# Column tiles on TensorE for two products of a gated attention kernel, with its work list laid out anew

## The chip, the cores and the metric

The kernel runs on one core of one Trainium2 chip. A time is the device time of one execution in microseconds (us). The profile comes from one execution, and its span runs from the first to the last instruction of the program.

A core has five engines that run side by side, each taking its own instructions in order: TensorE (PE in the profile; its loads of stationary operands, called weights here, are shown apart as PEld), VectorE (DVE), ScalarE (ACT), GpSimd (POOL) and SyncE (SP), which here only issues transfers. TensorE writes its results to PSUM, a memory of eight banks for each of 128 partitions, and another engine has to carry them from there to the large on-chip memory before the bank is used again.

## What is computed

There are two attention layers over the same input `x` (2048 tokens, 640 features, 32 heads of 20), and a gate for each token that mixes them. Layer A is a linear attention with softmax features of both signs:

```python
pk = einsum('bhsd,hdf->bhsf', k, w_phi)
phi_k = concatenate([softmax(pk), softmax(-pk)], axis=-1)
kv = einsum('bhsf,bhsd->bhfd', phi_k, v)
z = einsum('bhsf->bhf', phi_k)
num = einsum('bhqf,bhfd->bhqd', phi_q, kv)
den = einsum('bhqf,bhf->bhq', phi_q, z)[..., None] + 1e-06
a = (num / den) @ wo
```

Layer B works in four segments of 512 tokens. Within a segment it is causal softmax attention; beside it, features of the queries read a memory of the earlier segments, and both are mixed by a gate for each head. The result is `g * a + (1 - g) * b`. The change touches only `kv` and `z` of layer A.

## The kernel before

All matrices lie with 128 rows in the partitions. The key features of layer A are in `phk`, a tile of 128 x (16 token chunks, 640 features, 2 signs) in bf16, so that the features of one sign are every second element. The values of layer A are in `vA` (16 chunks x 640).

Every piece of work is a short function with numbered steps. The order is one hand-over list of words, `ORDER` (before: lines 838 to 898): the first letter names the function, the first digit its step, a second digit the PSUM bank, and an `a` that ScalarE carries the result from PSUM in place of VectorE. The loop behind the list calls the functions word by word, and as program order is kept on each engine, the list fixes the order in which each engine and each transfer queue works. Buffers and the waits between engines follow from the tiles that the steps read and write.

The words that matter here:

- `A` and `B`: key features and values of layer A, chunk by chunk. `B` reads the weights `WvA`.
- `S` (function `sums`, L357): `z` in blocks. The reference sums 2048 features in bf16, and the kernel follows that rounding: sums over blocks of 32 tokens come from TensorE, and VectorE adds the 64 blocks in order. In step 0, each 128 x 128 piece of `phk` is the weights and `ind` (128 x 4, one column for each block of 32 rows) is streamed: 40 matmuls of 4 columns in a step, 160 in all, into `zb_ps`. Step 1 copies a sign's result to `zt`, with the features already in the partitions.
- `s` (`blocks`, L372): 35 small VectorE operations, the running sums `zh` over the blocks and what is made of them for the denominators (`HZ`).
- `X` (`products`, L384): `kv`. For each of five groups of 128 features and each sign, 16 matmuls (one for each token chunk) with 128 x 128 weights from `phk` and 140 or 160 columns of `vA`: all heads that the group's 128 features touch. A head mask `hm` then clears what belongs to other heads when VectorE copies `kv_ps` to `KV`.
- `P` (`scores`) and `U` (`attended_cols`): the scores of layer B (`st_ps`), their exponentials on ScalarE (`PT`), and the attended values. `U` already uses four column tiles: the output of head i goes to partitions 32 i to 32 i + 31 (`uv_ps`). Its result is turned by a transfer (`U2`, `uN`), whose first reader is a reciprocal on VectorE (`U3`, `rden`). From the fourth on, all scores use one group of four banks, so a score step waits for the exponential of the one before it.
- `k`, `v`, `q`, `f`: projections, `o`: output projections; `d` and `n`: denominators and numerators of layer A; `M`: the memory of layer B.

Until about 60 us the list holds mainly loads, `A` and `B`; the `S` and `X` steps lie between 67 and 96 us, among the first score steps; then follow projections, scores and outputs until the end. `R0` closes the tiles of the first part, `phk`, `vA` and `WvA` among them, once `X` is done.

Of the kernel before, what the change touches and what calls it, by code (L numbers as in the profile page):

```python
# [8 lines left out]
ALU = mybir.AluOpType  # L9
# [6 lines left out]
def kernel(  # L16
# [192 lines left out]

    gps.memset(Msb, 0.0)  # L210
# [7 lines left out]
    ind = const.tile([P, 4], BF16, name="ind")  # L218
# [5 lines left out]
    zt = apool.tile([P, 2 * KC, 2, 32], BF16, name="zt")  # L224
# [9 lines left out]
    def item(kind, n):  # L234
        if (kind, n) not in items:
            items[kind, n] = It()
        return items[kind, n]
# [69 lines left out]
    def masks(n, step, at, ev):  # L307
        if step == 0:
            vec.tensor_tensor(
                out=Wphi, in0=Wc[:, :, None, :].to_broadcast([P, KC, NW, DH]),  # L310
                in1=hn_f[:, :, :, None].to_broadcast([P, KC, NW, DH]), op=ALU.mult)
            return
        if step == 1:
            vec.tensor_copy(out=hm, in_=hn_f)
        elif step == 2:
            vec.tensor_copy(out=ind, in_=bd01)
        else:
            vec.tensor_copy(out=HZ[:, :, step - 3, 0, :], in_=hm)
# [37 lines left out]

    def sums(n, step, at, ev):  # L357
        sgn, half = divmod(n, 2)
        t = item("S", sgn)
        if step == 0:  # L360
            if half == 0:
                t.ps = bank([P, KC, 4 * NCH], "zb_ps", at)
            for sc in range(half * NCH // 2, (half + 1) * NCH // 2):
                for c in range(KC):
                    ten.matmul(t.ps[:, c, 4 * sc:4 * sc + 4], lhsT=phk[:, sc, c * P:(c + 1) * P, sgn],
                               rhs=ind, start=(sc == 0 and c == 0),
                               stop=(sc == NCH - 1 and c == KC - 1), skip_group_check=True)
        else:
            vec.tensor_copy(
                out=zt[:, sgn * KC:(sgn + 1) * KC].rearrange("p c h k -> p c (h k)"), in_=t.ps)  # L370

    def blocks(n, step, at, ev):  # L372
        if n == 0:
            vec.tensor_copy(out=zh, in_=zt[:, :, :, 0])
        elif n < 32:
            vec.tensor_tensor(out=zh, in0=zh, in1=zt[:, :, :, n], op=ALU.add)
# [7 lines left out]
    def products(n, step, at, ev):  # L384
# [3 lines left out]
        if step == 0:  # L388
            t.ps = bank([P, hi - lo, DH], "kv_ps", at)
            for sc in range(NCH):  # L390
                ten.matmul(t.ps, lhsT=phk[:, sc, c * P:(c + 1) * P, sgn],
                           rhs=vA[:, sc, lo * DH:hi * DH],
                           start=(sc == 0), stop=(sc == NCH - 1))
# [423 lines left out]
    def tail_out(j, step, at, ev):  # L817
# [15 lines left out]
    WHICH = {**{f"V{j}": lambda i: i + UL for j in range(5)}, "k2": lambda i: 2 * i + 1, "o2": lambda i: 2 * i + 1, "S1": lambda i: 2 * i + 1,  # L833
# [103 lines left out]
```

## Time and profile before

| | us |
|---|---|
| median of 3 runs (291.45 to 294.0) | 291.5 |
| the profiled execution | 292.36 |
| its span | 290.6 |
| VectorE busy | 239.8 |
| ScalarE busy | 239.6 |
| GpSimd busy | 183.8 |
| busy with `zb_ps` (160 matmuls, 67.7 to 78.8 us) | 4.6 |
| busy with `kv_ps` (160 matmuls, 81.3 to 95.7 us) | 11.2 |

Engines work at the same time, so busy times are not added. A matmul's recorded length includes the time until its result has left the array, and the next one starts long before: what a step costs on TensorE is read from the distance of the starts, which the chain of work shows as the length of a piece. The clock granted to TensorE is 1.00 of full speed in all of the span.

### The profile page before, as it was taken

How to read it: one execution, taken by the hardware profiler on the slowest of the kernel's cores; microseconds unless marked ns; L12 is line 12 of the kernel's file. 1: busy time of each engine (PE TensorE's matmuls, PEld its weight loads, DVE VectorE, ACT ScalarE, POOL GpSimd, SP SyncE). 2: the span in 40 equal slices, each digit the busy share in tenths (PEclk: the TensorE clock that was granted, in tenths of full speed). 3: DMA queues.
4: the chain of work that ended last, by engine and by line, in shares of the span. 5: the costliest groups of instructions: out<-in, count | busy, mean ns of one | idle time of the engine just before them, and what ended most of it. 6: DMA issues, size and time to landing. Idle time of an engine off the chain costs nothing.

```text
span 290.6 us, 8207 instructions
## 1 busy us (share of the span) xinstructions
PE 278.1 (96%) x3233; PEld 176.2 (61%) x3233; DVE 239.8 (83%) x576; ACT 239.6 (82%) x260; POOL 183.8 (63%) x305
## 2 busy tenths in 40 slices
PE   8999999999999999999999999999999999898994
PEld 4676666667677546565546556556555555566673
DVE  5969999999699539999889988798898769989613
ACT  2478976998867899999999988999899998888801
POOL 8050000037346846797996899989789996998610
PEclk9999999999999999999999999999999999999999
DMA  7999960100110694546243425141736114356422
GB/s 226 252 237 215 166 142 11 36 2 20 20 20 20 203 158 89 72 86 134 39 92 72 106 58 104 39 106 36 124 72 139 26 41 111 83 122 126 106 62 90
DMA packets 79591, 28.10 MB, mean 97 GB/s; under 512 B 69952, under 2 KB 79552, under 8 KB 79552
## 3 DMA queue, kind: packets, MB, share of 16 engines
q1 hardware_dynamic: 78608, 26.84, 45.3%
q10 hardware_dynamic: 944, 0.74, 0.8%
q8 instruction: 25, 0.41, 0.6%
q14 instruction: 14, 0.11, 0.1%
HBM read 5.61 MB, written 2.62 MB: 28 GB/s over the span
## 4 chain that ended last, share of the span: by engine, by line
PE 66%; ACT 18%; DMA 5%; DVE 4%; POOL 3%; issue 3%; DVEq 0%; ACTq 0%; SPq 0%; POOLq 0%
ACT PT L117 15%; PE o_ps L117 9%; PE proj L117 8%; PE v_ps L117 8%; PE k_ps L117 8%; PE st_ps L117 7%; PE pf_ps L117 6%; PE q_ps L117 6%; PE uv_ps L117 4%; PE kv_ps L117 4%; DMA phk<-in_A_wqkv_dram 3%; PE mem_ps L117 2%; PE num_ps L117 2%; ACT ET L117 2%; PE zb_ps L117 1%
## 5 line engine op out<-in xcount | busy, mean ns | idle before, releaser
L117 ACT ACTIVATE PT<-st_ps 128x2048 bf16<-128x2048 f32 (+1 forms) x83 | 151.2, 1826 | 18.5 <-PE st_ps L117 14.0
L117 POOL TENSOR_SCALAR_AFFINE_SELECT PT<-PT 128x512 bf16<-128x512 bf16 (+2 forms) x116 | 80.5, 708 | 37.7 <-ACT PT L117 37.2
L117 PEld LDWEIGHTS <-xT 128*128 128x128 bf16 x640 | 59.5, 98 | 28.4 <-issue 5.7
L117 PE MATMUL st_ps<-qTp,kTs 32*128 32x384 bf16 (+3 forms) x512 | 31.8, 300 | 5.0 <-ACT PT L117 4.7
L117 ACT ACTIVATE Ek<-k_ps 128x640 bf16<-128x640 f32 x32 | 26.2, 893 | 6.2 <-PE k_ps L117 4.3
L117 POOL TENSOR_TENSOR Msb<-Msb,mtmp 128x84 f32<-128x84 f32 x24 | 9.3, 386 | 33.9 <-DVE mtmp L117 33.7
L117 DVE TENSOR_TENSOR t<-num_ps,dd 128x320 f32<-128x320 f32 x64 | 28.0, 481 | 2.3 <-POOL oA L117 1.3
L117 POOL TENSOR_TENSOR oA<-t,t 128x320 bf16<-128x320 f32 x32 | 29.1, 914 | 0.9 <-DVE t L117 0.7
L117 PEld LDWEIGHTS <-oT 128*128 128x128 bf16 x240 | 22.2, 98 | 10.4 <-issue 2.2
L117 PEld LDWEIGHTS <-kTs 32*128 32x128 bf16 (+1 forms) x552 | 14.8, 92 | 20.3 <-issue 16.3
L117 PE MATMUL proj<-WvB,xT 128*128 128x320 bf16 x160 | 26.2, 300 | 0.2 <-ACT vB L117 0.2
L117 PE MATMUL proj<-WkB,xT 128*128 128x320 bf16 x160 | 25.9, 300 | 0.0
L117 PE MATMUL q_ps<-xT,WqB 128*128 128x512 bf16 x100 | 24.9, 380 | 0.0
L117 PE MATMUL pf_ps<-xT,WqA 128*128 128x512 bf16 x100 | 24.9, 379 | 0.0
L117 PE MATMUL v_ps<-WvA,xT 128*128 128x320 bf16 (+1 forms) x160 | 24.5, 300 | 0.0
L117 PE MATMUL k_ps<-qTp,xT 128*128 128x320 bf16 x160 | 23.7, 299 | 0.1
L117 DVE TENSOR_REDUCE ksum<-Ek 128x64 f32<-128x1280 bf16 x16 | 23.3, 1455 | 0.0
L117 ACT ACTIVATE ET<-pf_ps 128x512 bf16<-128x512 f32 x40 | 22.0, 627 | 0.0
L117 POOL TENSOR_TENSOR oB<-td,tm 128x320 bf16<-128x320 f32 (+4 forms) x25 | 20.8, 835 | 0.4
L117 PE MATMUL o_ps<-WoA,oT 128*128 128x320 bf16 x120 | 20.3, 300 | 0.3 <-DVE tm L117 0.3
L117 PE MATMUL uv_ps<-PT,vB 128*32 128x512 bf16 (+1 forms) x448 | 20.4, 302 | 0.1
L117 PEld LDWEIGHTS <-phk 128*128 128x128 bf16 x370 | 17.6, 98 | 4.4 <-DMA phk<-in_A_x_dram 1.7
(115 smaller groups left out, 490.0 us busy)
## 6 DMA issues: line engine op xcount, KB each, us to landing
out_dram<-osb SPq DMA_DIRECT2D x12, 160.0 KB
qTp<-qd SPq DMA_DIRECT2D x8, 128.0 KB
WvB<-in_B_wv_dram SPq DMA_DIRECT2D x1, 800.0 KB
vA<-in_B_wq_dram SPq DMA_DIRECT2D x1, 800.0 KB
WvA<-in_A_wqkv_dram SPq DMA_DIRECT2D x1, 800.0 KB
WoA<-in_A_wo_dram SPq DMA_DIRECT2D x1, 800.0 KB
WoB<-in_B_wo_dram SPq DMA_DIRECT2D x1, 800.0 KB
qTp<-qd SPq DMA_DIRECT2D x8, 96.0 KB
```

What stands on the lines that cost most here:

```text
L117: return lambda *a, **k: kept(f(*a, **k))
```

## The change

It has three parts.

**Block sums.** The roles are exchanged: `ind` becomes the weights and `phk` is streamed, 320 features of one sign at a time. There are four steps (two halves of the features, two signs) with 16 matmuls each, in four column tiles: chunk 4 q + u goes to column tile q, that is to partitions 32 q to 32 q + 31, and the weights of u are 32 columns of which only 4 u to 4 u + 3 are not zero, so that four chunks add up into the same tile without touching each other's rows. Now the blocks are in the partitions and the features along the row, so the result goes to `zb` and one transfer turns it to `zt` (step 2). Both take the place of `WvA`, which is not needed any more by then. The running sums read other columns of `zt`.

```diff
+    ind = apool.tile([P, 144], BF16, name="ind")
+    gps.memset(ind, 0.0)
...
+    WvF = WvA.rearrange("p c n -> p (c n)")
+    zb = WvF[:, 0:2 * D].rearrange("p (s n) -> p s n", s=2)
+    zt = WvF[:, 2 * D:4 * D].rearrange("p (c n) -> p c n", n=P)
+    ztv = zt.rearrange("p c (h k) -> p c h k", h=2)
...
-            vec.tensor_copy(out=ind, in_=bd01)
+            vec.tensor_copy(out=ind.rearrange("p (u k) -> p u k", k=36)[:, :, 0:4],
+                            in_=bd01[:, None, :].to_broadcast([P, 4, 4]))
...
     def sums(n, step, at, ev):
+        if step == 2:
+            syn.dma_start_transpose(out=zt, in_=zb.rearrange("p s n -> p (s n)"))
+            return
         sgn, half = divmod(n, 2)
-        t = item("S", sgn)
-        if step == 0:
-            if half == 0:
-                t.ps = bank([P, KC, 4 * NCH], "zb_ps", at)
-            for sc in range(half * NCH // 2, (half + 1) * NCH // 2):
-                for c in range(KC):
-                    ten.matmul(t.ps[:, c, 4 * sc:4 * sc + 4], lhsT=phk[:, sc, c * P:(c + 1) * P, sgn],
-                               rhs=ind, start=(sc == 0 and c == 0),
-                               stop=(sc == NCH - 1 and c == KC - 1), skip_group_check=True)
-        else:
-            vec.tensor_copy(
-                out=zt[:, sgn * KC:(sgn + 1) * KC].rearrange("p c h k -> p c (h k)"), in_=t.ps)
+        t = item("S", n)
+        if step == 0:
+            t.ps = bank([P, 320], "zb_ps", at)
+            for u in range(4):
+                for q in range(4):
+                    ten.matmul(t.ps[32 * q:32 * q + 32, :], lhsT=ind[:, 32 * u:32 * u + 32],
+                               rhs=phk[:, 4 * q + u, half * 320:(half + 1) * 320, sgn],
+                               start=(u == 0), stop=(u == 3), tile_position=(0, 32 * q),
+                               skip_group_check=True)
+        else:
+            ev(out=zb[:, sgn, half * 320:(half + 1) * 320], in_=t.ps)
```

**Products.** Each 128 x 128 matmul of `X` becomes two with 64 columns of weights, in two column tiles (partitions 0 to 63 and 64 to 127 of the result). Each streams only the heads that its 64 features touch, 80 columns; the first chunk still streams all 140 or 160, which sets the whole region.

```diff
             for sc in range(NCH):
-                ten.matmul(t.ps, lhsT=phk[:, sc, c * P:(c + 1) * P, sgn],
-                           rhs=vA[:, sc, lo * DH:hi * DH],
-                           start=(sc == 0), stop=(sc == NCH - 1))
+                for f in range(c * P, (c + 1) * P, 64):
+                    a, b = (lo, hi) if sc == 0 else (f // DH, -(-(f + 64) // DH))
+                    r = f - c * P
+                    ten.matmul(t.ps[r:r + 64, a - lo:b - lo, :], lhsT=phk[:, sc, f:f + 64, sgn],
+                               rhs=vA[:, sc, a * DH:b * DH], start=(sc == 0), stop=(sc == NCH - 1),
+                               tile_position=(0, r), skip_group_check=True)
```

**The list.** All 1,600 words are put in a new order. Besides the `S` words the same steps are in it as often; some results are carried by another engine (four of `o` and two of `q` go from ScalarE to VectorE; one of `T`, one of `v` and two of the last outputs `h` go the other way, and ScalarE carries one of the four block sums). The part around the new steps, in which `S2` is the new transfer and `s0` a running sum:

```diff
-        "q2 B03 B3a A3 P1 B12 P2 S00 P3 B4 A5 B2a P4 P01 G0 B3a k01 B4 A4 P1 G1 B03 A5 P2 P3 B12 "
-        "G2 k1 B2 S0 K0 P4 G3 B3a K1 B4 P01 O0 S1 U01 P1 B03 U1 B12 U2 B2 G0 P3 P00 G1 S00 B3a B4 "
-        "G2 P1 G3 B01 B13 B2 P3 P00 U3 B3 S0 P1 B4 U4 B02 U5 S1 B11 s0 B2 P3 s0 P00 B3 U03 B4 s0 "
-        "s0 X00 s0 P1 U1 s0 U2 X02 s0 X1 s0 s0 s0 P3 P00 s0 X01 P1 X1 X03 s0 X1 s0 s0 s0 U3 P3 "
...
+        "P1 B4 B11 B2 U00 B3 B4 P3 P00 U1 J0 S03 P1 J4 U2 J1 B02 J2 J3 J5 B11 B2a O0 P3 P00 B3 "
+        "S00 S1a B4 P1 S02 U3 S1 U4 S01 U5 S1 U03 S1 G0 P3 P00 S2 U1 X00 P1 G1 G2 X02 G3 X1 X01 "
+        "X1 P3 P00 X1 M03 P1 f00 M6 U2 M7 k02 s0 s0 s0 s0 P3 P00 k1 X01 P1 s0 X03 U3 s0 X1 U4 s0 "
+        "U5 U02 s0 G0 X1 P3 P00 s0 X01 U1a G1 s0 G2 P1 s0 G3 U2 s0 X03 X1 s0 s0 X02 s0 X1 s0 s0 "
```

More of the change, by code (lines that the diff above doesn't have):

```diff
@@ L217 @@
     hm = const.tile([P, KC, NW], BF16, name="hm")
-    ind = const.tile([P, 4], BF16, name="ind")
     rgS = const.tile([P, NCH], F32, name="rgS")
@@ L223 @@
     CM = const.tile([P, G, 4, DH + 1], BF16, name="CM")
-    zt = apool.tile([P, 2 * KC, 2, 32], BF16, name="zt")
+    WvF = WvA.rearrange("p c n -> p (c n)")
+    zb = WvF[:, 0:2 * D].rearrange("p (s n) -> p s n", s=2)
+    zt = WvF[:, 2 * D:4 * D].rearrange("p (c n) -> p c n", n=P)
+    ztv = zt.rearrange("p c (h k) -> p c h k", h=2)
     zh = apool.tile([P, 2 * KC, 2], BF16, name="zh")
@@ L357, in sums @@
     def sums(n, step, at, ev):
+        if step == 2:
+            syn.dma_start_transpose(out=zt, in_=zb.rearrange("p s n -> p (s n)"))
+            return
         sgn, half = divmod(n, 2)
-        t = item("S", sgn)
+        t = item("S", n)
         if step == 0:
-            if half == 0:
-                t.ps = bank([P, KC, 4 * NCH], "zb_ps", at)
-            for sc in range(half * NCH // 2, (half + 1) * NCH // 2):
-                for c in range(KC):
-                    ten.matmul(t.ps[:, c, 4 * sc:4 * sc + 4], lhsT=phk[:, sc, c * P:(c + 1) * P, sgn],
-                               rhs=ind, start=(sc == 0 and c == 0),
-                               stop=(sc == NCH - 1 and c == KC - 1), skip_group_check=True)
-        else:
-            vec.tensor_copy(
-                out=zt[:, sgn * KC:(sgn + 1) * KC].rearrange("p c h k -> p c (h k)"), in_=t.ps)
+            t.ps = bank([P, 320], "zb_ps", at)
[5 more added lines that the diff above has]
+                               skip_group_check=True)
+        else:
+            ev(out=zb[:, sgn, half * 320:(half + 1) * 320], in_=t.ps)
     def blocks(n, step, at, ev):
         if n == 0:
-            vec.tensor_copy(out=zh, in_=zt[:, :, :, 0])
+            vec.tensor_copy(out=zh, in_=ztv[:, :, :, 0])
         elif n < 32:
-            vec.tensor_tensor(out=zh, in0=zh, in1=zt[:, :, :, n], op=ALU.add)
+            vec.tensor_tensor(out=zh, in0=zh, in1=ztv[:, :, :, 32 * (n // 16) + n % 16], op=ALU.add)
         elif n == 32:
@@ L832 @@
                  p=tail_first, a=tail_mid, e=tail_next, z=tail_last)
-    WHICH = {**{f"V{j}": lambda i: i + UL for j in range(5)}, "k2": lambda i: 2 * i + 1, "o2": lambda i: 2 * i + 1, "S1": lambda i: 2 * i + 1,
+    WHICH = {**{f"V{j}": lambda i: i + UL for j in range(5)}, "k2": lambda i: 2 * i + 1, "o2": lambda i: 2 * i + 1,
              **{f"M{j}": lambda i: i + G for j in range(2, 6)}, "p1": lambda i: 3 * i}
     ORDER = (
[60 rows of a table removed]
[61 rows of a table added]
     done = {}
```

113 rows, old and new, of the table ORDER are left out of this document.

## The prediction, as it was put on record

> **What bounds the kernel now.** I read the busy shares first, then the same busy times cut into four stages, then the chain of work that ended last, then the groups of instructions with their shapes apart, and the waits last. The profiled execution took 292.36 us (span 290.6 us and 1.76 us around it). The median of the three runs is 291.5 us, 0.86 us less, so a saving found in this profile is taken off 291.5.
>
> ```profile
> PE 278.1 (96%) x3233; PEld 176.2 (61%) x3233; DVE 239.8 (83%) x576; ACT 239.6 (82%) x260; POOL 183.8 (63%) x305
> ...
> PE 66%; ACT 18%; DMA 5%; DVE 4%; POOL 3%; issue 3%; DVEq 0%; ACTq 0%; SPq 0%; POOLq 0%
> ```
>
> ```profile
> core 0: us, PE busy (x) PEld busy (x) DVE busy (x) ACT busy (x) POOL busy (x), PEclk, DMA share, GB/s
> 0.00:20.00 20.00, 18.23 (x144) 12.32 (x145) 15.09 (x34) 9.57 (x16) 9.57 (x24) 1.00 0.95 245
> 20.00:110.00 90.00, 89.84 (x990) 59.98 (x989) 76.06 (x170) 73.95 (x102) 29.73 (x50) 1.00 0.47 86
> 110.00:274.00 164.00, 157.17 (x1975) 94.76 (x1977) 143.93 (x363) 152.99 (x140) 141.78 (x229) 1.00 0.43 87
> 274.00:290.60 16.60, 12.84 (x132) 9.18 (x131) 4.73 (x12) 3.04 (x4) 2.76 (x5) 1.00 0.22 67
> ```
>
> TensorE is what sets the end. It is busy 278.1 of 290.6 us, and its 12.5 us of idle time lie in three places: 1.8 us in the first 20 us (first loads), 6.8 us from 110 to 274, and 3.8 us behind the last matmul and in the tail. From 20 to 110 us, where both steps that the change rewrites lie, it is idle for 0.16 us. So work taken off TensorE there moves everything after it. From 110 to 274 us ScalarE is nearly as full (152.99 of 164, 93%), so there the time of either counts.
>
> The chain shows the steps in order (start, length, engine and output, matmuls):
>
> ```profile
> 69.96 1.37 PE v_ps L117 x10
> 71.32 0.98 PE zb_ps L117 x40
> 72.30 0.33 PE st_ps L117 x4
> 72.63 0.66 PE uv_ps L117 x16
> 73.29 1.47 PE v_ps L117 x10
> 74.76 0.33 PE st_ps L117 x8
> 75.09 1.09 PE zb_ps L117 x40
> ...
> 81.35 2.05 PE kv_ps L117 x32
> 83.40 0.33 PE st_ps L117 x8
> 83.73 2.05 PE kv_ps L117 x32
> ...
> 86.37 1.11 PE kv_ps L117 x16
> ...
> 88.57 2.19 PE kv_ps L117 x32
> ...
> 91.09 1.08 PE kv_ps L117 x16
> ...
> 93.84 2.05 PE kv_ps L117 x32
> ```
>
> Three prices come out of it. A block-sum matmul (`zb_ps`) costs 0.98/40 = 24.5 ns although it streams only 4 columns: that is what one load of 128x128 weights with one short matmul takes, and it also says that such a load fits into 24.5 ns. Steps that change the way the array is divided cost about 0.10 us more (`v_ps` 1.47 before a score step against 1.37 before a block-sum step, `zb_ps` 1.09 against 0.98). And `uv_ps`, which already runs as four column tiles, streams 512+384+256+128 = 1280 columns in each tile in 0.66 us: one tile after the other would be 5120 columns, so the four run side by side, at 0.56 us and one change of 0.10.
>
> **Block sums, part by part.** Before, 160 matmuls in four groups: 4 x 0.98 = 3.9 us, without changes of division. After, four steps of 16 matmuls, four tiles side by side with 4 x 320 = 1280 columns each, the same as `uv_ps`: 4 x 0.56 = 2.2 us. In the new list three of the four stand between a score step and a `uv_ps` step, with no change more; the first stands between a score step and a value projection, one change more, 0.1. Together 2.3, a saving of 1.6 us. The streamed operand is now every second element of `phk`; no row shows such a stream. If it went at half rate the steps would take 4.5 us, 0.6 more than before; I take full rate, because the only rows with this stride (`phk` as weights, below) show loads as quick as those without it, and keep 2.2 us in the range.
>
> ```profile
> L117 PE MATMUL zb_ps<-ind,phk 128*128 128x4 bf16 x160 | 4.6, 164 | 0.0
> ...
> L117 PEld LDWEIGHTS <-xT 128*128 128x128 bf16 x640 | 59.5, 98 | 28.4 <-issue 5.7 <-DVE osb L117 0.2
> ...
> L117 PEld LDWEIGHTS <-phk 128*128 128x128 bf16 x370 | 17.6, 98 | 4.4 <-DMA phk<-in_A_x_dram 1.7 <-issue 1.5 <-DMA phk<-in_A_wqkv_dram 0.8
> ...
> L117 PEld LDWEIGHTS <-vB 128*32 128x32 bf16 x448 | 9.5, 96 | 11.1 <-issue 3.1 <-DVE t L117 1.1 <-DVE rden L117 0.3
> ```
>
> The evacuation grows from two casts to three on VectorE and one on ScalarE:
>
> ```profile
> L117 DVE CAST zt<-zb_ps 128x320 bf16<-128x320 f32 x2 | 1.0, 489 | 0.9 <-PE zb_ps L117 0.9
> ```
>
> That is 0.49 us more on VectorE, which is idle 90 - 76.1 = 14 us between 20 and 110 us; nothing on the path. The new transfer that turns the sums goes into SP's queue behind the first `uN` transfer and ahead of the second; it waits for the last of the four casts, which stands just ahead of it in the list. The nearest transfer takes 2.86 us for 512 columns:
>
> ```profile
> 118.16 2.86 DMA uN<-uT
> ```
>
> For 1280 columns that is 2.86 us if its length doesn't matter and 7.2 us if it goes by columns. Between it and the first running sum the list puts three products, a score step, a memory step, a feature projection and a key projection, about 4.8 us of TensorE's work. So VectorE's queue, with the product evacuations behind those sums, waits 0 to 2.4 us; I take 0, since from 512 to 1280 columns the fixed part stays, and keep 2.4. The result is wanted by the denominators some 25 us later. The clear of the larger `ind` is one short memset on an idle GpSimd.
>
> **The products.** Before: 2.05 x 3 + 2.19 + 1.11 + 1.08 = 10.5 us, of which six changes of division are 0.6: 9.9 us for 160 matmuls, 62 ns each. After: 320 matmuls, in 16 rounds of two tiles for each of ten products, 80 columns instead of 140 (all 140 or 160 in the first round). A round lasts as long as the longer of its stream and its weight load. The stream:
>
> ```profile
> 211.43 0.32 PE num_ps L117 x6
> ```
>
> Six matmuls of 4 x 140 + 2 x 80 = 720 columns in 0.32 us are 0.44 ns a column, 36 ns for 80 columns. The load is the unknown: 64 columns of weights into each of two tiles, while no row shows a column tile whose stream is short enough to show its load. Lower end: hidden, 36 ns. Middle: a round issues two pairs of a load and a matmul, and 24.5 ns is the shortest turn of such a pair in any row, so 49 ns if the two tiles' pairs follow one another. Upper end: each of the two loads takes twice the whole 128-column load, 98 ns. The ten products then take 10 x (16 x r + 0.03): 6.1, 8.1 or 16.0 us. I take 49 ns, since a turn bound by its load is what `zb_ps` shows and `uv_ps` with its long streams doesn't, so 8.1 us and a saving of 1.8 us; the ends are a saving of 3.8 and a loss of 6.1.
>
> [...]
>
> **The list.** The steps of TensorE are the same in number apart from these two kinds, so the new list can change the end only by TensorE's idle time.
>
> ```profile
> L117 ACT CAST qd<-q_ps 128x512 bf16<-128x512 f32 x8 | 4.7, 586 | 0.0
> ...
> L117 ACT CAST osb<-o_ps 128x320 bf16<-128x320 f32 x8 | 3.4, 425 | 0.5 <-PE o_ps L117 0.5
> ```
>
> It gives VectorE six copies that ScalarE had (4 of `osb`, 2 of `qd`), 0.43 and 0.59 us each, about 3 us, taken from an engine at 93% and put on one with 20 us idle in the same stage. It puts the score steps at the same distance: by the step lengths of the chain some 192 us of TensorE's work lie between the fourth and the last of 80 in the old list, 2.5 us for each. In the tail TensorE has no gap after 278.14 in either list, but the last evacuation goes from two casts in a row to one:
>
> ```profile
> 278.14 8.17 PE o_ps L117 x60
> 286.34 0.89 DVE vB L117 x2
> ```
>
> That is 0.3 us less, since the last matmul runs beside the first of the two. For 110 to 274 us I take the idle time as it is, 6.8 us; what a new list can win or lose there I put at 2.5 us either way, about a third of it.
>
> Sum: -1.6 (block sums) -1.8 (products) -0.3 (last evacuation) = -3.7 us; 292.36 becomes 288.7, and the median 291.5 - 3.7 = 287.8 us.
>
> **Rivals.** First, another bound takes the place of TensorE. The score steps share one group of four banks, so each waits for the exponential before it:
>
> ```profile
> PE st_ps L117 <- ACT PT L117: 4.7, 16, 0.6
> ...
> DVE rden L117 <- DMA uN<-uT: 3.6, 2, 3.3
> ```
>
> ```profile
> L117 ACT ACTIVATE PT<-st_ps 128x2048 bf16<-128x2048 f32 x77 | 145.4, 1888 | 18.3 <-PE st_ps L117 14.0 <-PE uv_ps L117 1.3 <-POOL Mbd L117 0.6
> ```
>
> One turn is 1.89 + 0.40 us and hand-overs, 2.4 us, and the list has 2.5 us of TensorE's work for it. If quicker products only lengthen that wait, 1.8 us are lost again: 289.6 us. For it speaks ScalarE's 93%, against it that in the products' stage ScalarE still has 90 - 74 = 16 us idle. Chance 0.27.
>
> Second, slower: the new list reads the turned columns sooner. Adding TensorE's steps between a `uN` transfer and its reader (the reciprocal `rden` on VectorE), the median over 28 units falls from 3.5 to 2.9 us and now meets the 2.86 us of the transfer. A reader that comes too early stops VectorE, with key, value and numerator evacuations queued behind it, and then TensorE's banks. With half of the units late by 0.5 us that is 7 us: 287.8 + 7 = 294.8 us. It decides once VectorE, idle 12% of that stage, reaches the reader before the landing; the old list shows it twice, for 3.6 us. Chance 0.13.
>
> Third, slower: weight loads in column tiles are not hidden behind the streams, or are twice as long. Then a round is 36 + 49 = 85 to 98 ns, the products take 13.9 to 16.0 us, and the time is 291.5 - 1.6 - 0.3 + 4.0 to 6.1 = 293.6 to 295.7 us. [...] Against it stand these rows of the plain and the tiled form, loads beside the matmuls of the same rows:
>
> ```profile
> 72.56 0.50 PEld L117 LDWEIGHTS <-vB 128*32 128x32 bf16 x16 [0.23 <-DVE omgb L117]
> 72.56 0.73 PE L117 MATMUL uv_ps<-PT,vB 128*32 128x512 bf16 x16
> ```
>
> Chance 0.10.
>
> **The numbers.** The forecast has 0.50. Its own range is 284.5 (loads hidden, a little less idle) to 289.5. A measurement of this kernel can tell about 1% from no change, 2.9 us: faster means under 288.6, slower over 294.4. Faster: 0.45 of the forecast and 0.03 of the first rival. Within 1%: 0.05 and 0.24, and 0.05 of the two slow cases near their lower ends. Slower: 0.18. The range leaves out the upper half of the slow cases and a few in a hundred below: 284.5 to 294.5.
>
> **What would show it.** `zb_ps` as four groups of 16 at 0.55 to 0.66 us, and `kv_ps` at 32 matmuls in 0.8 to 0.9 us a product, say the terms are right; 0.6 says the loads are hidden, 1.4 or more is the third rival. TensorE idle between 110 and 274 us well over 6.8 us, with VectorE waiting for `uN`, is the second; a wait of scores for exponentials well over 4.7 us is the first. A running sum waiting for its transfer, or block sums at twice 0.56, would break the cover or the stream rate that I assumed.

## The result and the profile after

The changed kernel takes 293.86 us (median of 20 runs, 291.92 to 295.81) against 291.71 us for the kernel before (20 runs beside it). The ratio is 1.0063, with a 95% interval of 1.0045 to 1.0080: about 2 us slower, where 3.7 us less were forecast. Its profiled execution took 293.18 us with a span of 291.5 us. The two profiled executions lie only 0.8 us apart (292.36 and 293.18), so the traces hold less than half of the 2.15 us between the two medians; where the rest lies is not shown.

The busy times of the engines and the chain's shares by engine, after:

```profile
PE 273.7 (94%) x3276; PEld 171.0 (59%) x3297; DVE 242.4 (83%) x579; ACT 240.1 (82%) x259; POOL 183.0 (63%) x306
...
PE 58%; ACT 20%; DVE 7%; DMA 5%; POOL 4%; issue 3%; SPq 1%; DVEq 0%; ACTq 0%; POOLq 0%
```

The groups of instructions of the two rewritten steps, and their pieces on the chain (start, length, matmuls):

```profile
L117 PE MATMUL kv_ps<-vA,phk 128*64 128x80 bf16 (+1 forms) x320 | 7.0, 203 | 0.0
...
L117 PE MATMUL zb_ps<-phk,ind 128*32 128x320 bf16 x64 | 2.6, 305 | 0.0
```

```profile
72.85 0.68 PE zb_ps L117 x15
75.32 1.83 PE zb_ps L117 x43
...
82.84 1.35 PE kv_ps L117 x64
```

Both rewritten operations do what was hoped, the products more. Three block-sum steps take 1.83 us, so four take 2.5 us (2.3 forecast; 4.1 before, with its two changes of division; the chain counts 58 of the 64 matmuls). Two products take 1.35 us, 0.10 of it a change of division: 0.62 us each, or (0.62 - 0.03) / 16 = 37 ns a round of two tiles, close to the lower end of the forecast's bounds (36 ns). The busy time of `kv_ps` falls from 11.0 us (11.2 where its two shapes are added up) to 7.0 us and that of `zb_ps` from 4.6 to 2.6.

TensorE's busy time falls by 4.4 us, but the span grows by 0.9: its idle time went from 12.5 to 17.8 us. The same stages as before, with one more, 110 to 120 us, that lies inside the third (columns as in the prediction: TensorE, weight loads, VectorE, ScalarE, GpSimd, granted clock, DMA share, GB/s):

```profile
0.00:20.00 20.00, 18.43 (x145) 12.55 (x146) 14.90 (x31) 8.74 (x15) 10.09 (x25) 1.00 0.96 247
20.00:110.00 90.00, 87.08 (x1061) 55.42 (x1068) 78.71 (x173) 78.48 (x108) 28.00 (x45) 1.00 0.48 92
110.00:120.00 10.00, 7.79 (x103) 4.56 (x104) 7.99 (x20) 6.66 (x6) 6.56 (x14) 0.83 0.46 63
110.00:274.00 164.00, 155.10 (x1906) 93.44 (x1919) 142.83 (x361) 148.02 (x132) 141.21 (x232) 0.99 0.47 85
274.00:291.50 17.50, 13.09 (x168) 9.58 (x166) 5.96 (x16) 4.83 (x6) 3.69 (x6) 1.00 0.28 70
```

From 20 to 110 us TensorE now stands for 2.92 us where it stood for 0.16; from 110 to 274 for 8.90 where it stood for 6.83; and from 110 to 120 us its clock is 0.83 on average. TensorE's waits name the first places (engine, operation, whom it waited for: total, times, longest):

```profile
PE st_ps L117 <- ACT PT L117: 5.3, 16, 0.7
PE dn_ps L117 <- DVE uT L117: 2.4, 1, 2.4
...
PE uv_ps L117 <- DVE kpads L117: 0.9, 2, 0.6
PE pf_ps L117 <- DVE qd L117: 0.7, 1, 0.7
```

And VectorE waits for the turned columns `uN` eight times, where it waited twice before (3.6 us in all, 3.3 the longest):

```profile
DVE rden L117 <- DMA uN<-uT: 8.2, 8, 3.0
```

Follow TensorE's wait of 2.4 us back. SP's queue before and after around it (start, length in the queue, operation):

```profile
96.25 0.47 SPq L117 DMA_DIRECT2D WoA<-in_A_wo_dram  x1
96.77 0.51 SPq L117 DMA_DIRECT2D WoB<-in_B_wo_dram  x1
98.22 1.57 SPq L117 DMA_DIRECT2D qTp<-qd  x2
99.83 1.48 SPq L117 DMA_TRANSPOSE kTs<-kpads  x1
101.35 1.56 SPq L117 DMA_DIRECT2D qTp<-qd  x2
103.09 1.20 SPq L117 DMA_TRANSPOSE uN<-uT  x1
```

```profile
97.30 0.41 SPq L117 DMA_DIRECT2D WoA<-in_A_wo_dram  x1
97.76 1.71 SPq L117 DMA_DIRECT2D WoB<-in_B_wo_dram  x1
99.51 4.97 SPq L117 DMA_TRANSPOSE kTs<-kpads  x2
104.59 2.25 SPq L117 DMA_DIRECT2D qTp<-qd  x3
106.94 5.63 SPq L117 DMA_TRANSPOSE uN<-uT  x2
```

In both kernels the two 800 KB loads of the output weights go out at 96 to 98 us, and five smaller transfers stand between them and the next `uN`. The old list has two copies of queries first, 1.45 us behind the second load; in the new list two transfers of keys stand directly behind it. The second load and the two key transfers now hold the queue for 6.7 us, the three copies for 2.3, and `uN` is issued 9.2 us behind the second load instead of 6.3. The cast that fills `uT` for that transfer ended at 103.0 us, 3.9 us before the issue, so it is the queue that holds it. Then the chain of waits and the timeline of the changed kernel read:

```profile
106.94 3.48 DMA uN<-uT
```

```profile
110.52 0.25 DVE L117 RECIPROCAL rden<-uN 128x16 f32<-128x16 bf16 x1 [3.05 <-DMA uN<-uT]
110.69 0.63 DVE L117 CAST uT<-uv_ps 128x512 bf16<-128x512 f32 x1
...
111.37 1.20 PE L117 MATMUL dn_ps<-HZ,ET 128*128 128x16 bf16 x40 [2.35 <-DVE uT L117]
```

VectorE stands for 3.05 us before the reciprocal; the next `uT` cast behind it comes late; TensorE, whose next matmuls want the bank that this cast empties, stands for 2.35 us. Straight after, from 111.6 us, the records show a granted clock of 0.50 for 3.4 us, which, as an estimate, can cost up to another 1.7 us. The mean clock of a run tells, as an estimate, how often that happened: one such window in 291.5 us leaves a mean of 1 - 1.7 / 291.5 = 0.994. Of the 20 runs of the changed kernel 19 have a mean of 0.985 to 0.994 and took 292.28 to 295.81 us; the one at 1.000 took 291.92. The kernel before shows it too, but seldom: of its 92 runs beside the experiments 12 have a mean of 0.994 and took 292.91 to 293.64 us, with a median of 293.2, the other 80 a median of 291.7 (five of these took 293.65 to 293.93 at 1.000, without a window). So one window goes with some 1.5 us there, and the change makes it common, not new.

The second place is VectorE's queue behind the new transfer of the block sums:

```profile
82.93 0.66 DVE L117 COPY zh<-WvA 128x20 bf16<-128x20 bf16 x1 [1.92 <-DMA WvA<-WvA]
83.62 0.65 DVE L117 TENSOR_TENSOR zh<-zh,WvA 128x20 bf16<-128x20 bf16 x3
84.19 0.48 DVE L117 CAST kpads<-proj 128x320 bf16<-128x320 f32 x1
...
84.73 0.73 PE L117 MATMUL uv_ps<-PT,vB 128*32 128x512 bf16 x16 [0.56 <-DVE kpads L117]
```

The transfer was issued at 77.77:

```profile
77.77 1.35 SPq L117 DMA_TRANSPOSE WvA<-WvA  x1
```

The first sum reads it at 82.93; VectorE waits 1.92 us for it, the key copy behind the sums is late, and TensorE stands for 0.56 us. Behind that, from 84 to 97 us, VectorE catches up. That stretch before and after:

```profile
84.00:97.00 13.00, 12.96 (x203) 10.02 (x201) 10.75 (x40) 9.85 (x6) 7.37 (x14) 1.00 0.13 26
```

```profile
84.00:97.00 13.00, 11.44 (x252) 6.83 (x249) 12.49 (x52) 10.11 (x9) 5.87 (x13) 1.00 0.21 44
```

VectorE is busy for 12.49 of 13 us, so here it is the bound, and TensorE loses 1.56 us: the 0.56 us at 84 us, 0.69 us at 95 us behind a copy of queries (`qd` in the list of waits), and smaller gaps.

### The profile page after: what moved, and what is told of

Read it like the earlier page. It is cut to its first block, busy times and chain, and to the rows that moved or that the text cites. A ratio compares the mean times of both kernels' runs of the same rounds, so it can differ in the third digit from the quotient of the medians.

```text
span 291.5 us, 8325 instructions
## 1 busy us (share of the span) xinstructions
PE 273.7 (94%) x3276; PEld 171.0 (59%) x3297; DVE 242.4 (83%) x579; ACT 240.1 (82%) x259; POOL 183.0 (63%) x306
## 4 chain that ended last, share of the span: by engine, by line
PE 58%; ACT 20%; DVE 7%; DMA 5%; POOL 4%; issue 3%; SPq 1%; DVEq 0%; ACTq 0%; POOLq 0%
ACT PT L117 17%; PE o_ps L117 9%; PE proj L117 8%; PE v_ps L117 8%; PE k_ps L117 8%; PE st_ps L117 7%; PE pf_ps L117 5%; PE q_ps L117 4%; DMA uN<-uT 4%; PE uv_ps L117 3%; DVE zh L117 2%; POOL PT L117 2%; PE num_ps L117 2%; DMA WkB<-in_B_wk_dram 2%; PE mem_ps L117 2%
## 5 line engine op out<-in xcount | busy, mean ns | idle before, releaser
L117 POOL TENSOR_SCALAR_AFFINE_SELECT PT<-PT 128x512 bf16<-128x512 bf16 (+2 forms) x116 | 79.4, 698 | 66.6 <-ACT PT L117 64.9
L117 ACT ACTIVATE Ek<-k_ps 128x640 bf16<-128x640 f32 x32 | 27.0, 894 | 5.2 <-ACT vA L117 1.8
L117 PE MATMUL proj<-WkB,xT 128*128 128x320 bf16 x160 | 26.5, 300 | 0.4 <-DMA WkB<-in_B_wk_dram 0.4
L117 PE MATMUL pf_ps<-xT,WqA 128*128 128x512 bf16 x89 | 24.3, 380 | 1.5 <-DVE qd L117 0.7
L117 POOL TENSOR_TENSOR oB<-td,tm 128x320 bf16<-128x320 f32 (+4 forms) x25 | 20.2, 811 | 1.8 <-DVE tm L117 0.8
L117 PEld LDWEIGHTS <-ET 128*128 128x128 bf16 x352 | 16.5, 98 | 7.4 <-issue 5.1
L117 PE MATMUL o_ps<-WoB,oT 128*128 128x320 bf16 x120 | 20.2, 299 | 0.0
```

The source lines that it names most:

```text
L117: return lambda *a, **k: kept(f(*a, **k))
```

## The experiments

Ratios are to runs of the kernel before on the same chip, with 95% intervals. The letters of theories are those of the expectations.

**x_old: the products alone, in the old list.** The kernel before, with only the products' diff:

```diff
-                ten.matmul(t.ps, lhsT=phk[:, sc, c * P:(c + 1) * P, sgn],
-                           rhs=vA[:, sc, lo * DH:hi * DH],
+                for f in range(c * P, (c + 1) * P, 64):
+                    a, b = (lo, hi) if sc == 0 else (f // DH, -(-(f + 64) // DH))
+                    r = f - c * P
+                    ten.matmul(t.ps[r:r + 64, a - lo:b - lo, :], lhsT=phk[:, sc, f:f + 64, sgn],
```

> The kernel before, list and block sums untouched; only the products run as two column tiles. If TensorE's work sets the end here (theory A, the prediction's own): the products fall from 10.5 to about 6.1 us in the chain, as in the changed kernel, and the time falls by 3.8 to 287.9 us. If the exponentials and VectorE are as much of a bound (theory B): the same 6.1 us for the products, but more TensorE idle time behind them, and 290 to 291.5 us.

Measured: 292.15 us, ratio 0.9998 (0.9977 to 1.0019). The products cost less, and the time stays, to within 0.6 us either way. The stretch from 78 to 98 us, which had 19.96 us of TensorE's work before, and the waits of TensorE in it:

```profile
78.00:98.00 20.00, 17.12 (x489) 12.04 (x487) 15.61 (x60) 15.02 (x8) 11.86 (x22) 1.00 0.21 29
```

```profile
PE st_ps L117 <- ACT PT L117: 2.9, 5, 0.7
```

Five of the eight score steps in the stretch wait for the exponential of the one before: the first rival, with its mechanism, in the old list. TensorE stands for 2.88 us there, and of the products' saving nothing shows in the time, though ScalarE is idle a quarter of the stretch. What counts is the turn of one score group, 2.4 us (four exponentials in a row start at 81.18, 83.56, 86.01 and 88.44 us), not ScalarE's share.

**old_new: the list alone, with the old operations.** The new order of words, with the old 128 x 128 products and the old four-column block sums (split by features over the four `S` steps, `S2` empty).

```diff
         if step == 0:
-            t.ps = bank([P, 320], "zb_ps", at)
+            t.ps = bank([P, KC, 4 * NCH], "zb_ps", at)
...
+            for sc in range(NCH):
+                for c in cs:
+                    ten.matmul(t.ps[:, c, 4 * sc:4 * sc + 4], lhsT=phk[:, sc, c * P:(c + 1) * P, sgn],
+                               rhs=ind, start=(sc == 0 and c == cs[0]),
```

> The new list with the old operations: 128 x 128 products and block sums with the features as weights (the same four steps, without the transfer). If the new list lost the time by its waits wherever TensorE idles, and TensorE's work adds on top (theory A): 293.9 + 5.4 = 299.3 us. If the work fits into the gaps that the new list leaves (theory B): 293.5 to 296 us.

Measured: 299.1 us, ratio 1.0234 (1.0169 to 1.0299). The list is 7 us worse for the old operations, as theory A says. Two windows of half clock lie in its trace (from 79.6 us, 0.51 up to 83.0 us, and from 117.2 us; the mean is 0.989), which, as an estimate, can cost up to 3.4 of the 7 us. The list is laid out for the new operations, and a list can't be judged apart from the operations that it was made for.

**both_old and both_old2: both operations, in the old list.** The old words, with the new steps put at the places of the old ones. The block sums and their turned copy lie in two work buffers (`Ek`) in place of `WvA`, which the old list still reads there. In `both_old` one group of block sums stands ahead of key features that it reads, so its sums are of unfinished data; `both_old2` has them in the right order.

```diff
-        "... P2 P3 B12 G2 k1 B2 S0 K0 P4 G3 B3a K1 B4 P01 O0 S1 U01 P1 B03 U1 B12 ..."
+        "... P2 P3 S00 B12 G2 k1 B2 S1 K0 P4 G3 B3a K1 B4 P01 O0 S00 U01 P1 B03 U1 S1 B12 ..."
```

> Block sums and products as in the changed kernel, in the old list; only the steps that the new block sums need are moved (each half is copied out before the next one starts, and the first five running sums stand behind the transfer). Theory A: 291.7 - 3.8 - 1.6 = 286.3 us. Theory B: 289 to 291.5 us. If the new operations themselves cost what the changed kernel lost (theory C, for instance the turned sums coming late): 293 us or more.

> New block sums and products in the old list, with all four block-sum steps behind the last key features (in both_old the first one read features that were not there yet). Theory B, that the old list has no work ready to take the place of what is saved: between 291.5 and 296 us, TensorE idle more than in the kernel before by nearly what its work is less. Theory A: 286.3 us.

Measured: 295.75 us, ratio 1.0113 (1.0058 to 1.0168), and 293.74 us, ratio 1.0047 (1.0020 to 1.0075). Without a new list the two operations together, with those buffers, make the kernel slower. The waits of TensorE from 78 to 98 us in `both_old2`:

```profile
PE st_ps L117 <- ACT PT L117: 1.8, 3, 0.7
PE kv_ps L117 <- DVE uT L117: 1.3, 1, 1.3
PE kv_ps L117 <- DVE KV L117: 0.7, 1, 0.7
PE mem_ps L117 <- DVE KV L117: 0.3, 1, 0.3
```

Beside the exponentials, more than half of it is now waiting for VectorE. VectorE waits 1.9 us for the new transfer in this run and gets its products faster; that these, and not the buffers, make it late was not tested apart.

**wo_later: both loads of output weights behind the late transfer.** In the changed kernel:

```diff
-        syn.dma_start(out=lt.WoA, in_=rows5(A_wo))
-        syn.dma_start(out=lt.WoB, in_=rows5(B_wo))
+        if step == 2:
+            syn.dma_start(out=lt.WoA, in_=rows5(A_wo))
+            syn.dma_start(out=lt.WoB, in_=rows5(B_wo))
+            return
...
-        "U1 f01 q2 v1 U2 v02 f1 P3 P00 v1 f2 M00 ..."
+        "U1 f01 q2 v1 U2 R2 v02 f1 P3 P00 v1 f2 M00 ..."
```

> The changed kernel, but the two loads of the output weights are issued behind the first uN transfer that follows them in the list instead of ahead of two key transfers and three query transfers. If that queue makes the uN transfer late (theory D): VectorE's 3.0 us wait at 107 us goes, TensorE's 2.4 us gap at 109 us with it, the granted clock stays at 1.00 where it was 0.83, and the time falls by about 4 us to 289.9. If the key and query transfers alone hold it back: the wait shrinks by less than 1 us and the time stays within 1 us of 293.9.

Measured: 292.12 us, ratio 0.9997 (0.9970 to 1.0024), 1.9 us less than the changed kernel (0.9997 against 1.0063). The forecast of theory D was 289.9. The stop at 109 us is gone, and the same thing happens one transfer later, for which VectorE waits 1.76 us:

```profile
109.98 5.65 DMA uN<-uT
```

**wo_split: the loads in ten pieces.** Two pieces of 160 KB behind each of the first five `uN` transfers after the denominators begin:

```diff
+        if step == 2:
+            W, w = ((lt.WoA, A_wo), (lt.WoB, B_wo))[n % 2]
+            syn.dma_start(out=W[:, n // 2, :], in_=rows5(w)[:, n // 2, :])
+            return
...
-        "... v00 P3 P1 U2 K1 v03 d6 ..."
+        "... v00 P3 P1 U2 R2 R2 K1 v03 d6 ..."
```

> The changed kernel with the output weights in ten pieces of 160 KB, two behind each of five uN transfers after the first denominators, in place of two loads of 800 KB in a row. Theory D says that the late uN transfers are all that the stretch from 107 to 120 us lacks: waits of VectorE for uN fall from 8.2 us to under 3.6, which the kernel before has, TensorE's gaps between 109 and 120 us fall under 0.8 us together, and the time falls by 3.5 us to 290.4. If the same wait comes back elsewhere, as behind the two late loads (292.1): 291.5 to 292.5 us.

Measured: 290.68 us, ratio 0.9960 (0.9932 to 0.9988), 3.0 us less than the changed kernel, with a mean clock of 0.997 to 1.000 in nine of ten runs. So the changed kernel is slower than the kernel before with the two loads where the new list has them, and faster with them in pieces behind the transfers. Theory D was right about the time (290.4) and not about all of the waits: VectorE's waits for `uN` fall from 8.2 to 6.9 us and not under 3.6, and TensorE's idle time from 109 to 120 us falls from 3.19 to 1.23 us and not under 0.8. But none of TensorE's waits from 100 to 125 us is for VectorE any more. The kernel before was not run with its loads in pieces, so what the same edit would gain there is not known.

**filler: the clock by itself.** The changed kernel with 16 matmuls that nobody reads in the stop of 2.35 us, so that the stop stays and TensorE is busy in it:

```diff
+    def filler(n, step, at, ev):
+        ps = item("M", done["M0"] - 1).ps
+        for i in range(16):
+            ten.matmul(ps[:, 0:4, :], lhsT=xT[:, 0, 0:P],
...
-        "U3 M02 U1 P1 M01 k03 U4 M6 U5 U2 M6 d00 ..."
+        "U3 M02 U1 P1 M01 k03 g0 U4 M6 U5 U2 M6 d00 ..."
```

> The changed kernel plus 16 matmuls of 336 columns into unused columns of a bank that is held anyway, put into TensorE's queue just ahead of the denominators, where it waits 2.35 us at 109 us. They cost no time as long as they fit into that wait. If the halved clock that follows the wait (0.50 for 3.4 us from 111.6) is a second part of the loss (theory E): the clock stays at 1.00, the score marks between the 15th and the 18th lose 2 us instead of 3.7, and the time falls by about 1.5 us to 292.4. If the clock costs nothing, since other engines are waited for in that stretch: within 0.5 us of 293.9, or later by what doesn't fit.

```profile
108.87 2.44 PE L117 MATMUL mem_ps<-xT 128*128 128x336 bf16 x16
```

Measured: 292.7 us, ratio 1.0033 (1.0006 to 1.0059), with a clock of 0.997 to 1.000 in nine of ten runs. The stop is filled by those 2.44 us and TensorE does its work no earlier, yet its median ratio is 0.0030 lower, 0.9 us, though the two intervals overlap. That fits the half clock's upper bound of 1.7 and is less than the 1.5 us that went with a window in the kernel before. As an estimate, 0.9 to 1.5 of the 3.0 us that `wo_split` gains are then the clock, and the rest is the stop.

**zh_cut, s_later, s_pool: VectorE's queue.** In `zh_cut` 24 of the 32 running sums are left out, so the denominators lack blocks 4 to 27. In `s_later` the first four sums stand behind the key copy. In `s_pool`, which has that too, GpSimd adds every second block into an accumulator of its own, which rounds otherwise.

```diff
+        elif 4 <= n < 28:
+            return
```

```diff
-        "X1 P3 P00 X1 M03 P1 f00 M6 U2 M7 k02 s0 s0 s0 s0 P3 P00 k1 X01 ..."
+        "X1 P3 P00 X1 M03 P1 f00 M6 U2 M7 k02 P3 P00 k1 s0 s0 s0 s0 X01 ..."
```

```diff
+        elif n == 1:
+            gps.tensor_copy(out=zg, in_=ztv[:, :, :, 1])
+        elif n < 32 and n % 2:
+            gps.tensor_tensor(out=zg, in0=zg, in1=ztv[:, :, :, 32 * (n // 16) + n % 16], op=ALU.add)
```

> The changed kernel without 24 of its 32 running sums on VectorE (blocks 4 to 27 are left out of the denominators): some 6 us of VectorE work less between 84 and 96 us. If VectorE's row of sums and product copies holds TensorE back there (theory F): TensorE's gaps at 84, 88 and 95 us (0.56, 0.15 and 0.69) close, the score marks keep the lead of 3 us that they have at the 8th up to the 14th, and the time falls by 1.5 to 3 us. If the score turns hold it: less than 0.5 us.

> The changed kernel with its first four running sums put behind the copy of the keys (list word k1) that follows them, nothing else. In the changed kernel VectorE waits 1.9 us for the new transfer in front of the first sum, the key copy behind it comes late, and TensorE stands for 0.56 us at 84.2 us. Theory S (the transfer that the prediction took at nothing costs that stop): the stop at 84 us goes, and the time is 0.5 to 0.6 us under the changed kernel's, about 293.2. Theory B (VectorE is the bound from 84 to 97 us, sums included): the 0.56 us come back as a longer stop before 97 us or as a longer wait at 109 us, since the loads of the output weights set that one; 293.6 to 294.0.

> As the run before, and every second of the running sums goes to GpSimd, in an accumulator of its own, added to VectorE's at the end: 16 of VectorE's operations less. Theory B: with VectorE relieved both stops before 97 us go (0.56 and 0.69 us), though the wait at 109 us on the late weight loads may eat part: 292.7 to 293.4. Theory G: GpSimd, which masks the scores' triangles and multiplies the attended values in the same stretch, is delayed by its 16 additions of some 0.2 us each and passes it on: 293.8 to 295.

Measured: 293.13 us (1.0042, 1.0007 to 1.0076), 293.64 us (1.0062, 1.0039 to 1.0085) and 291.47 us (0.9985, 0.9959 to 1.0010). The stretch from 84 to 97 us in the first and the third:

```profile
84.00:97.00 13.00, 12.01 (x248) 7.04 (x252) 8.54 (x27) 10.10 (x10) 7.44 (x13) 1.00 0.26 56
```

```profile
84.00:97.00 13.00, 12.75 (x255) 7.33 (x248) 8.74 (x34) 10.67 (x10) 10.80 (x29) 1.00 0.29 59
```

`zh_cut` frees VectorE, and the stop at 95 us is gone. But it leaves the wait for the transfer where it was (2.0 us), and with it the stop at 84 us, so TensorE still loses 0.99 us. By the ratios it gains 0.6 us, which the intervals don't tell from nothing, where theory F forecast 1.5 to 3.

`s_later` removes the stop at 84 us, and it doesn't come back in this stretch: TensorE is busy for 12.21 of the 13 us there. VectorE's work stays as long as it was (12.48 us), and the stop of 0.62 us at 95 us stays with it, as does the stop of 2.4 us behind the late `uN`. The ratio is that of the changed kernel (1.0062 for 1.0063), with intervals of 0.7 us either way. So the 0.56 us of theory S do not show in the time, but these runs can't rule them out.

Only the two edits together give TensorE 12.75 of 13 us, and `s_pool` is 2.2 us under `s_later`, clear of both intervals. That is more than the 0.9 us forecast for it at best, and more than what it saves in this stretch. GpSimd's 15 additions took 235 ns each there, for the some 0.2 us of theory G. Of the 1.9 us by which TensorE's idle time differs between the two profiled executions, 0.54 us lie from 84 to 97 us and 1.5 us behind 274 us; why the end is shorter too was not traced.

**best1 and best2: both mended, with fewer pieces.** `wo_split` with `s_later` (`best1`) and with `s_pool` (`best2`), and the pieces behind the first, second, third, fifth and sixth transfer.

> The changed kernel with the output weights in ten pieces of 160 KB, two behind each of five transfers of the attended values (the fourth such transfer after the denominators begin is passed over, since the earlier run with pieces there had a stop of 0.99 us behind it against 0.32 us), and with the first four running sums behind the key copy. Theory S and D together: 290.7 us of the run with ten pieces, less 0.56 us at 84 us and 0.67 us at 140 us: about 289.5, a ratio of 0.993. If the stop at 84 us only moves: 290.1.

> As the run before, and every second running sum on GpSimd. If VectorE is what stops TensorE at 95 us (0.70 us in the run with ten pieces): 288.8 us, a ratio of 0.990. If GpSimd is delayed by it, or if the scores' exponentials take over there: 289.5 to 290.5.

Measured: 291.82 us (1.0003, 0.9993 to 1.0014) and 290.60 us (0.9961, 0.9948 to 0.9973), 2.3 and 1.8 us over the forecasts. The timeline of `best2` shows most of it, and `best1` has the same wait of 1.8 us: the last pieces now come too late for the first output product.

```profile
147.52 0.57 SPq L117 DMA_DIRECT2D WoA<-in_A_wo_dram  x1
150.01 0.30 PE L117 MATMUL o_ps<-WoA,oT 128*128 128x320 bf16 x1 [1.80 <-DMA WoA<-in_A_wo_dram]
```

**half_pool and half_pool3: do the losses add up?** The pieces of `wo_split`, the sums of `s_later`, and blocks 16 to 31 added on GpSimd in the same accumulator and order, so that the rounding is the reference's again; `half_pool3` places the pieces as 3, 3, 3, 0 and 1.

```diff
-            vec.tensor_tensor(out=zh, in0=zh, in1=ztv[:, :, :, 32 * (n // 16) + n % 16], op=ALU.add)
+            (vec if n < 16 else gps).tensor_tensor(out=zh, in0=zh, in1=ztv[:, :, :, 32 * (n // 16) + n % 16], op=ALU.add)
```

> The changed kernel with three edits: the output weights in ten pieces, two behind each of the first five transfers of attended values after the denominators begin; the first four running sums behind the key copy; and the running sums of blocks 16 to 31 on GpSimd instead of VectorE, in the same accumulator and in the same order, so that the rounding of the sums stays. If the three losses add up (late transfers, VectorE's queue before 97 us, the rest of the list's idle time as in the run with ten pieces): 290.7 us of the run with ten pieces, less 0.2 us that putting the sums later gave there, less 0.5 to 0.8 us for the halved sums: 289.7 to 290.0. If the saving of the sums is swallowed behind them by the exponentials: 290.4 or more.

> As the run before, with the pieces as 3, 3, 3, 0 and 1 behind the same five transfers. If the stop of 0.99 us at 140 us comes from the two pieces issued behind the fourth transfer: 0.6 us less than the run before, and no wait of an output product for its weights, since the last piece is issued behind the fifth transfer as there. If nine pieces in the first three intervals slow their transfers instead: stops at 116 to 126 us, and the same time as the run before or more.

Measured: 289.44 us (0.9921, 0.9890 to 0.9951) and 290.15 us (0.9937, 0.9916 to 0.9958). The time of `half_pool` is 0.3 us under what adding up the losses gives, and it beats both kernels. Its interval (0.9 us either way) overlaps that of `wo_split`, though, so the 1.1 us that the two other edits seem to add are not shown for certain. Its stages from 84 us and its longest waits of VectorE:

```profile
84.00:97.00 13.00, 12.69 (x270) 7.42 (x264) 8.30 (x33) 10.07 (x9) 8.96 (x26) 1.00 0.24 54
97.00:110.00 13.00, 12.43 (x160) 6.99 (x158) 10.36 (x21) 12.71 (x16) 9.70 (x19) 1.00 0.49 80
```

```profile
DVE rden L117 <- DMA uN<-uT: 5.5, 8, 1.6
```

`half_pool3` was wrong in its reason: with no piece behind the fourth transfer it still has a stop of 0.71 us at 139.5 us, and `half_pool`, with two pieces there, has none. Those pieces are not what causes that stop; what does stays open.

## Why the prediction was wrong, point by point

**What bounds the kernel.** That TensorE sets the end was right for the kernel before, and not a property of the stretch. Once 5 us of work had gone from it, VectorE (12.49 of 13 us) took over from 84 to 97 us in the new list, and the turn of the scores in the old one. The prediction read VectorE's idle time as an average, 14 us of the 90 from 20 to 110 us, while the running sums, product evacuations and copies fall into 13 of them.

**Block sums.** Right: 2.5 us for 2.3, and the operand with every second element does not stream at half rate (1.83 us for three steps of four rounds with 320 columns are 0.48 ns a column; `num_ps` has 0.44).

**Products.** The term was mis-sized: 37 ns a round and not 49, the hidden end of its bounds. Ten products of 0.62 us and some six changes of division are 6.8 us for the 10.5 before, 3.7 us saved and not 1.8. The third rival falls with it. The row of `uv_ps` pointed the right way: a round of two tiles takes 37 ns where its stream of 80 columns takes 36 by the 0.44 ns of `num_ps`, and its two loads, which use all rows, don't show in it.

**The new transfer.** The wait was bounded by 0 and 2.4 us and taken as 0; it is 1.92 us. The transfer took 5.2 us from its issue until its reader went on, between the bounds of 2.86 and 7.2. That a fixed part of it stays from 512 to 1280 columns, the reason for taking 0, was the author's estimate and not shown. The cover was mis-sized: 3.2 us and not 4.8. It was counted in TensorE's steps, but the reader stands in VectorE's queue, and VectorE had nothing left to do before the first sum from 81.01 us on, when it had made the memory step's copy; the copy of the key projection, whose work was counted in, stands behind the sums.

**The last evacuation.** The 0.3 us didn't come. The chain of the changed kernel ends with a cast of 0.43 us on ScalarE and one of 0.49 us on VectorE, one behind the other, as long as the two before (0.89 us).

**The list: the step that failed.** The prediction says that the new list can change the end only by TensorE's idle time, and takes that as it is from 110 to 274 us, with 2.5 us either way. That stage did stay inside (8.90 for 6.83 us). But 2.76 us came up from 20 to 110 us, for which nothing had been allowed, and 0.65 us behind 274 us; in all TensorE stands 5.3 us longer, more than the 4.4 us of work that it saves. The clock was taken as 1.00. SP's queue was read only around the new transfer: the loads of the output weights are not in the diff, but the new list puts two key transfers directly behind them, ahead of the next `uN`. Putting these loads in pieces behind the transfers took 3.0 us off, 0.9 to 1.5 of them, as an estimate, the half clock.

**The rivals.** The first is what happens to the products in the old list (`x_old`: 0.9998). The second had the right wait, VectorE's for `uN`, and nearly its size (8 waits of 8.2 us for 14 of 7 us), but another cause: the rival has the list read sooner, while the wait that stops TensorE, one of 3.05 us, comes from a transfer that leaves late.

The profiled execution of `half_pool` takes 289.38 us, 2.98 us under the 292.36 of the kernel before; by the ratio it is 2.3 us. That this comes near the 3.7 us of the sum doesn't bear the sum out. The sum has 1.8 us for products that saved 3.7 us of TensorE's time, `half_pool` has three edits that the prediction didn't have, and the kernel before was not run with the like. As far as these runs show, the nearness is chance.

## What to carry to other kernels

When an engine that sets the end gets quicker in one stretch, look at the queues of that stretch, not at stage averages: who has 13 us of work in those 13 us, and what do transfers stand behind. A list that is laid out anew moves bulk loads against small transfers even where the diff names neither (here `uN` left 9.2 us behind the second load and not 6.3); read each queue's order through, and put bulk loads in pieces behind the transfers that somebody waits for (3.0 us in `wo_split`). A stop of TensorE can be paid for twice, the second time by the clock: behind the stop of 2.35 us the clock was 0.50 for 3.4 us, and with the stop filled (`filler`) the mean was 0.997 to 1.000 in nine of ten runs.

## What was not expected of the hardware

The granted clock was 0.50 for 3.4 us after a single stop of 2.35 us. The length of the stop alone doesn't decide it: the same followed a stop of 1.16 us in `x_old` (halved from 247.7 us, a mean of 0.994) and one of 1.32 us in `both_old` (a mean of 0.994), while the clock stayed at 1.00 behind a stop of 1.17 us in the kernel before (up to 247.85 us), of 1.27 us in `both_old2` and of 1.80 us in `best2`. And a stop is not needed: in `old_new` the granted clock falls to 0.51 right behind 5.60 us without a gap of TensorE (153 matmuls, among them block sums with 4 streamed columns each):

```profile
74.00:79.60 5.60, 5.60 (x153) 4.28 (x151) 2.73 (x9) 3.22 (x5) 2.76 (x5) 1.00 0.35 26
79.60:83.00 3.40, 3.40 (x33) 3.40 (x31) 1.03 (x5) 1.88 (x1) 1.22 (x2) 0.51 0.20 39
```

What decides it was not tested.

A turning transfer (`uN`) that took 2.86 us in the kernel before (at 118.16 us) took 5.65 us in `wo_later` (at 109.98 us), issued 3.3 us behind the second of two 800 KB loads (that the loads are the cause was not tested apart). And a VectorE operation that takes 0.34 us at 112 us of the changed kernel took 1.98 us at 97 us, while GpSimd cleared a tile for 1.69 us (that the clearing is the cause is not shown):

```profile
96.83 1.98 DVE L117 TENSOR_SCALAR uk<-kpads 128x640 bf16<-128x640 bf16 x1
...
112.05 0.34 DVE L117 TENSOR_SCALAR uk<-kpads 128x640 bf16<-128x640 bf16 x1
```

```profile
96.94 1.69 POOL L117 MEMSET phik<- 128x1536 bf16 x1
```
